# Fourier convolution of a 224 x 224 x 96 image: inverse transform of segments 6 and 7 regrouped, nine sums moved to GpSimd, four halo copies to ScalarE

## The chip, the cores and the metric

The kernel runs on one core of one Trainium2 chip. Its time is device time in microseconds (us) of one execution; the median over runs is compared. The engines are PE (TensorE, matmuls; its weight loads are listed as PEld), DVE (VectorE), ACT (ScalarE), POOL (GpSimd) and SP (SyncE, which only issues DMAs here). Each engine works through its own queue in order.

## The reference

```python
# x: (1, 224, 224, 96) bf16, w: (7, 7, 96, 96) bf16
wp = jnp.pad(w, ((0, H - K), (0, W - K), (0, 0), (0, 0)))
Xf = rfft2(x, axes=(1, 2)); Wf = rfft2(wp, axes=(0, 1))        # float32
Yf = jnp.einsum('bhwi,hwio->bhwo', Xf, Wf)
y = irfft2(Yf, s=(H, W), axes=(1, 2)).astype(bfloat16)
```

This is a circular convolution of the image with a 7 x 7 filter, 96 channels in and 96 out.

## The kernel before, in words

The 224 rows are cut into 8 segments (`NJ`) of 28 output rows (`B`), each with 6 rows of overlap, so 34 rows (`L`). Along the rows the kernel uses a transform of length 34, as matmuls with the matrix `Fm` (forward, step A) and `G` (inverse, step C). It has 17 frequencies (`NS`); a frequency has two parts (`r`), which gives `FR` = 34 rows of `G` per segment. Along the columns the 7-tap filter is applied directly to pairs of columns (step B). The 224 columns are cut into 7 tiles of 32 columns, that is 16 pairs (`TW`).

**Step A**, `a_jobs(t)`: for tile t, matmuls of image rows with `Fm` into a PSUM bank, then an evacuation into `xf` (two buffers, tile t uses t % 2). `new_xf` first copies the last three column pairs of the tile before into the new buffer, the halo, in two copies of 96 x 816 elements.

**Step B**, `b_round(t, s)`: one frequency s of one tile. 33 small matmuls (96 columns) go into two banks b0 and b1. ACT writes `tt_` from b0, DVE forms `u` and `v` from `tt_`, b0 and b1, and a last sum `yf = v + u` (`ysum`) runs on DVE if `ydve` is set, else on POOL. `u`, `v` and `tt_` have two buffers each, so a round can't write `u` before the sum two rounds back has read it. The operands of the matmuls are planes `J`, sums of parts of `xf` that `jit(t, g)` makes on DVE for a group of three frequencies at a time, in a *burst*: three DVE instructions that are put into one round (`planes`). Where the sum of a burst round is on POOL, it is made to wait for the last of the planes ("sum after planes").

**Step C**, `c_jobs(t)`: `yf` goes to a DRAM scratch `scr` (`put_y`), is read back as `tt` with rows (segment, frequency, part) and columns (pair, channel) (`load_t`), is multiplied by `G` and evacuated into `yo`, which is written to the output. Three segments make a group of 102 rows and 84 output rows (3 x 28); the 8 segments are the groups `CG` = (0, 3), (3, 3), (6, 2). A tile has two halves h of 8 pairs; each half and group takes four matmuls of two pairs (384 columns), so 24 matmuls per tile, two per bank pair in a job q. Loads and outputs are issued on SP, in program order; six `tt` buffers (`NTT`) are filled by `pump` as jobs are done.

**Order of the work.** The program is written out in Python, and each engine keeps the order of emission. The steps for the filter (`prep_jobs(gi)`, matmuls from `wq` whose results go to `WF`, and `w_sub`, a DVE subtraction on `WF`) and step A and C jobs are queued with a first and a last position (`add(a, b, jobs)`); `pace` pops them at two places of each round. In phase 1 tiles 0 and 1 go side by side: round r holds the *sub-rounds* (r, 0) for tile 0 with s = r, and (r, 1) for tile 1 with s = r - 4 (`LAG`). Bursts stand in (6, 0), (7, 1), (9, 0), (10, 1), (12, 0), (13, 1), (15, 0), (17, 1) and (19, 1), and before those in (4, 1) and earlier. From tile 2 on a tile runs alone, beside step A of the next tile and step C of the one or two before; `CQ[t]` tells how many jobs of the older and of the newer tile fall into tile t. `evac` chooses DVE or ACT for each evacuation by two counters `load["v"]` and `load["a"]`. The last tile (`TL`) ends in a tail with its own inverse matmuls `GA` and `GB`; the remaining jobs of tile 5 run at its start.

Nearly all instructions carry the line 82 of a helper in the profile, so they are told apart by their tiles.

Of the kernel before, what the change touches and what calls it, by code (L numbers as in the profile page):

```python
# [14 lines left out]
B = 28  # L15
# [7 lines left out]
TW = 16  # L23
HALO = 3
PXC = 16
# [12 lines left out]
LAG = 4  # L38
CQ = {2: (12, 2), 3: (10, 5), 4: (7, 8), 5: (4, 11), 6: (1, 6)}
NXN = 2  # L40
NP2 = 0
# [8 lines left out]
def kernel(  # L50
# [338 lines left out]
    def new_xf(t):  # L389
        xf = xf_bufs[t % 2]  # L390
        xf_tiles[t] = xf
        if t > 0:
            prev = xf_tiles[t - 1]
            for ph in range(2):
                r = VE.tensor_copy(out=xf[0:C, ph, :, :, 0:HALO, :].rearrange("c r s w j -> c (r s) (w j)"),
                                   in_=prev[0:C, ph, :, :, TW:TW + HALO, :].rearrange("c r s w j -> c (r s) (w j)"))
                apart(("A", t), "halo", r)
        return xf
# [188 lines left out]

    def load_t(t, gi, h):
        j0, nj = CG[gi]
        n = nj * FR  # L590
        tt = t_pool.tile([128, TW // 2, 2 * C], BF16, name="tt")
        tt_tiles[(t, gi, h)] = tt
        sv = scr_tiles[t].rearrange("w j s (r e) -> (j s r) w e", r=2)
        n0 = n // 16 * 16
        for (p0, p1) in ((0, n0), (n0, n)):
            dma(tt[p0:p1], sv[j0 * FR + p0:j0 * FR + p1, h * 8:(h + 1) * 8])
# [21 lines left out]

    def c_jobs(t):
        jobs = []  # L620
        for h in range(2):
            for gi in range(3):
# [3 lines left out]
                def mk_(q, h=h, gi=gi, j0=j0, nj=nj, hold=hold):  # L626
                    def f():
                        if q == 0:
                            hold["yo"] = yo_pool.tile([4 * B, PXC * C], BF16, name="yo")
                        tt = tt_tiles[(t, gi, h)]  # L630
                        yo = hold["yo"]
                        if True:
                            pc = psum_tile() if NP2 else None
                            for b in range(2):
                                pb = pc[:, b] if NP2 else bank()
                                TE.matmul(pb[0:nj * B, 0:4 * C], lhsT=G[0:nj * FR, 0:nj * B],
                                          rhs=tt[0:nj * FR, 4 * q + 2 * b:4 * q + 2 * b + 2, :].rearrange("p w e -> p (w e)"), start=True, stop=True)
                                if not NP2:
                                    evac(yo[0:nj * B, (2 * q + b) * 4 * C:(2 * q + b + 1) * 4 * C], pb[0:nj * B, 0:4 * C], 4 * C)
                            if NP2:  # L640
                              evac(yo[0:nj * B, q * 8 * C:(q + 1) * 8 * C].rearrange("p (b e) -> p b e", b=2), pc[0:nj * B, :, 0:4 * C], 8 * C)
                        if q == 1:
                            w0 = t * 2 * TW + h * PXC
                            dma(out[0, j0 * B:(j0 + nj) * B, w0:w0 + PXC, :].rearrange("h w c -> h (w c)"), yo[0:nj * B])
                            held[0] -= 1
                            pump()
                    return f
                for q in range(2):
                    jobs.append(mk_(q))
# [65 lines left out]
    qs = []  # L715
# [5 lines left out]
    for gi in range(1, len(PGRP)):  # L721
        b0 = PGRP[gi][0]
        add(max(0, 2 * b0 - 10), 2 * b0 - 4 if gi > 1 else 1, prep_jobs(gi) if gi > 1 else p1)
        for h, (r, t) in enumerate(((max(b0 - 4, 2), 1), (b0 - 2, 0)) if gi > 1 else ((0, 0), (0, 0))):
# [14 lines left out]
    for r in range(NS + LAG):  # L739
# [4 lines left out]
        for t in range(2):  # L744
# [8 lines left out]
            b_round(t, s, fills(qs, 2 * r + (t if both else 0)), fills(qs, 2 * r + (t if both else 1)), bool(now), now)  # L753
# [133 lines left out]
```

## Time and profile before

| | |
|---|---|
| median of 13 runs | 288.1 us (286.7 to 288.88) |
| profiled execution | 286.84 us |
| its span | 285.1 us |
| PE busy | 264.9 us (93%) |
| DVE busy | 242.1 us (85%) |
| ACT busy | 185.3 us (65%) |
| POOL busy | 87.5 us (31%) |

Groups of instructions in the part of the page that lists the costliest ones (busy us, mean ns of one):

| engine, output and input | count | busy | mean |
|---|---|---|---|
| PE, pb from WF, J | 2898 | 166.5 | 206 |
| POOL, yf from v, u | 75 | 75.4 | 1018 |
| ACT, xf from pb (96 x 408 and smaller) | 139 | 60.9 | 482 |
| ACT, yo from pb (84 x 384 and smaller) | 130 | 55.9 | 479 |
| PE, pb from tt, Gm | 144 | 35.6 | 328 |
| DVE, yf from v, u | 36 | 20.6 | 571 |
| DVE, copies xf from xf | 12 | 9.0 | 789 |

A matmul's mean is longer than what it holds PE for, since matmuls overlap in the pipeline; the busy column counts the overlap once. Arrows in the answers ("<-") name what ended an idle time.

### The profile page before, as it was taken

To read this page: it belongs to the slowest core of one execution; us is meant where nothing else is said; L and a number is where in the kernel's file an instruction comes from. 1 tells how busy PE (TensorE), PEld (TensorE's weight loads), DVE (VectorE), ACT (ScalarE), POOL (GpSimd) and SP (SyncE) were. 2 spreads that over 40 slices of the span, in tenths; PEclk is the share of its full clock that TensorE was granted. 3 is DMA by queue.
4 is the path that set the end of the run, shared out by engine and by line. 5 is a ranking of instruction groups with operands and counts; after the bars stand their busy time and mean duration, and the time that the engine had idled before them with its cause. 6 is when DMAs were issued, how large, how long until landed. Compare 5 with 4: busy or idle time off the path is not lost.

```text
span 285.1 us, 11562 instructions
## 1 busy us (share of the span) xinstructions
PE 264.9 (93%) x4822; PEld 236.2 (83%) x4822; DVE 242.1 (85%) x523; ACT 185.3 (65%) x460; POOL 87.5 (31%) x122
## 2 busy tenths in 40 slices
PE   8499998999968889999999999999999999889992
PEld 3198898999968889888989888899989888888661
DVE  6279999999899999988977799778997889988833
ACT  5079885756522856886888767987688875265523
POOL 2741001223423333332243313422332235343300
PEclk9979999999999999999999999999999999999979
DMA  8687242111121369998768773786759832596875
GB/s 162 109 225 194 44 143 76 46 44 44 47 84 44 110 208 187 236 281 259 216 165 236 212 231 95 157 217 181 216 202 220 223 100 85 156 209 191 218 202 180
DMA packets 44492, 46.01 MB, mean 161 GB/s; under 512 B 33458, under 2 KB 35182, under 8 KB 44344
## 3 DMA queue, kind: packets, MB, share of 16 engines
q1 hardware_dynamic: 44024, 43.78, 58.1%
q10 hardware_dynamic: 416, 1.49, 2.3%
q8 instruction: 38, 0.62, 1.0%
q14 instruction: 14, 0.11, 0.1%
HBM read 23.92 MB, written 21.33 MB: 159 GB/s over the span
## 4 chain that ended last, share of the span: by engine, by line
PE 52%; DVE 26%; DMA 7%; issue 5%; ACT 4%; POOL 2%; SPq 0%; DVEq 0%; POOLq 0%; ACTq 0%
PE pb L82 52%; DVE J L82 9%; DVE v L82 5%; DMA wq<-in_w_dram 4%; DVE xf L82 3%; DVE yf L82 3%; DVE WF L82 2%; POOL yf L82 2%; DVE u L82 2%; ACT xf L82 2%; DMA xn<-in_x_dram 2%; ACT WF L82 1%; DMA tt<-scr 1%; DVE yo L82 1%; SPq L82 0%
## 5 line engine op out<-in xcount | busy, mean ns | idle before, releaser
L82 PE MATMUL pb<-WF,J 96*128 96x96 bf16 x2898 | 166.5, 206 | 6.1 <-DVE J L82 5.4
L82 PEld LDWEIGHTS <-J 96*128 96x128 bf16 (+1 forms) x2910 | 142.0, 98 | 20.7 <-issue 8.7
L82 POOL TENSOR_TENSOR yf<-v,u 128x384 bf16<-128x384 f32 x75 | 75.4, 1018 | 162.7 <-issue 90.8
L82 ACT CAST xf<-pb 96x408 bf16<-96x408 f32 (+1 forms) x139 | 60.9, 482 | 6.9 <-PE pb L82 4.5
L82 PE MATMUL pb<-WF,xf 96*128 96x96 bf16 x952 | 60.1, 206 | 0.7 <-DVE WF L82 0.6
L82 ACT CAST yo<-pb 84x384 bf16<-84x384 f32 (+1 forms) x130 | 55.9, 479 | 4.7 <-PE pb L82 4.2
L82 DVE TENSOR_TENSOR J<-xf 96x1824 bf16<-96x1824 bf16 (+1 forms) x84 | 57.2, 720 | 0.1
L82 PEld LDWEIGHTS <-xf 96*128 96x128 bf16 x952 | 47.1, 98 | 1.0 <-issue 0.7
L82 PE MATMUL pb<-Fm,xn 118*128 118x136 bf16 x448 | 46.4, 222 | 1.2 <-DVE u L82 0.8
L82 PE MATMUL pb<-tt,Gm 102*84 102x384 bf16 (+1 forms) x144 | 35.6, 328 | 1.4 <-DMA tt<-scr 1.0
L82 ACT CAST WF<-pb 96x480 bf16<-96x480 f32 (+1 forms) x58 | 29.9, 581 | 10.1 <-PE pb L82 9.9
L82 PEld LDWEIGHTS <-xn 118*128 118x128 bf16 x448 | 30.0, 98 | 2.6 <-issue 1.9
L82 PE MATMUL pb<-wq 98*128 98x120 bf16 (+1 forms) x288 | 23.8, 234 | 4.4 <-DMA xn<-in_x_dram 4.4
L82 PEld LDWEIGHTS <-wq 98*128 98x128 bf16 x288 | 21.1, 151 | 4.9 <-issue 4.9
L82 DVE TENSOR_TENSOR J<-J 96x912 bf16<-96x912 bf16 (+1 forms) x42 | 25.0, 596 | 0.0
L82 DVE TENSOR_TENSOR yf<-v,u 128x384 bf16<-128x384 f32 x36 | 20.6, 571 | 1.2
L82 DVE CAST xf<-pb 96x408 bf16<-96x408 f32 (+1 forms) x33 | 15.6, 513 | 0.2 <-PE pb L82 0.2
L82 PEld LDWEIGHTS <-Gm 102*84 102x84 bf16 (+1 forms) x144 | 11.8, 113 | 4.5 <-DMA tt<-scr 1.1
L82 PE MATMUL pb<-wu 128*128 128x512 bf16 (+1 forms) x48 | 13.2, 448 | 1.1 <-DVE ct L82 1.1
L82 DVE CAST WF<-pb 96x480 bf16<-96x480 f32 (+1 forms) x14 | 8.5, 612 | 6.0 <-PE pb L82 5.6
L82 PEld LDWEIGHTS <-wu 128*128 128x128 bf16 (+1 forms) x48 | 6.5, 137 | 7.6 <-issue 2.8
L82 DVE COPY xf<-xf 96x816 bf16<-96x816 bf16 x12 | 9.0, 789 | 0.0
(390 smaller groups left out, 215.8 us busy)
## 6 DMA issues: line engine op xcount, KB each, us to landing
xn<-in_x_dram SPq DMA_DIRECT2D x13, 672.0 KB
scr<-yf SPq DMA_DIRECT2D x30, 288.0 KB
tt<-scr SPq DMA_DIRECT2D x24, 288.0 KB
out_dram<-yo SPq DMA_DIRECT2D x24, 252.0 KB
tt<-scr SPq DMA_DIRECT2D x12, 192.0 KB
out_dram<-yo SPq DMA_DIRECT2D x12, 168.0 KB
scr<-yf SPq DMA_DIRECT2D x6, 192.0 KB
scra<-yf SPq DMA_DIRECT2D x3, 288.0 KB
```

The costliest lines, as they stand in the source:

```text
L82: r = fn(*a, **k)
```

## The change

Five things are changed together.

- Step C of segments 6 and 7: a group of two segments over 8 pairs becomes one over 6 pairs in each half, with 68 rows. The remaining 34 rows of each `tt` tile are filled with parts of the pairs 12 to 15 of segments 6 and 7 (`REST`): in the first half segment 6, pairs 12 to 15, and segment 7, pairs 12 and 13; in the second half segment 7, pairs 14 and 15. So the first half has three matmuls of three segments, and the second one of three and two of two segments: 22 matmuls per tile instead of 24, and the third group is one job instead of two. Loads and outputs of the added parts are DMAs of their own, on SP.
- `CQ` is written for 10 jobs per tile instead of 12.
- The sums of burst rounds go to POOL for r >= 4 in phase 1, behind the planes.
- The halo copies of tiles 2 and 3 are on ACT, and all halo copies are counted in `load`.
- The filter jobs of group 5 and its two `w_sub` come two positions (one round) later.

```diff
@@ -36,7 +36,7 @@
 YBUF = 4
 JGB = ((0, 3), (3, 6), (6, 9), (9, 12), (12, 15), (15, 17))
 LAG = 4
-CQ = {2: (12, 2), 3: (10, 5), 4: (7, 8), 5: (4, 11), 6: (1, 6)}
+CQ = {2: (10, 2), 3: (8, 4), 4: (6, 7), 5: (3, 9), 6: (1, 5)}
 NXN = 2
 NP2 = 0
 WARM = 16
@@ -392,7 +392,9 @@
         if t > 0:
             prev = xf_tiles[t - 1]
             for ph in range(2):
-                r = VE.tensor_copy(out=xf[0:C, ph, :, :, 0:HALO, :].rearrange("c r s w j -> c (r s) (w j)"),
+                hc = SE.copy if t in (2, 3) else VE.tensor_copy
+                load["a" if t in (2, 3) else "v"] += 850 if t in (2, 3) else 600
+                r = hc(out=xf[0:C, ph, :, :, 0:HALO, :].rearrange("c r s w j -> c (r s) (w j)"),
                                    in_=prev[0:C, ph, :, :, TW:TW + HALO, :].rearrange("c r s w j -> c (r s) (w j)"))
                 apart(("A", t), "halo", r)
         return xf
@@ -585,6 +587,8 @@
     tt_tiles = {}
     puts = []
 
+    REST = (((6, 12, 16, 0), (7, 12, 14, 4)), ((7, 14, 16, 0),))
+
     def load_t(t, gi, h):
         j0, nj = CG[gi]
         n = nj * FR
@@ -592,8 +596,12 @@
         tt_tiles[(t, gi, h)] = tt
         sv = scr_tiles[t].rearrange("w j s (r e) -> (j s r) w e", r=2)
         n0 = n // 16 * 16
+        w0, w1 = (h * 8, (h + 1) * 8) if gi < 2 else (h * 6, (h + 1) * 6)
         for (p0, p1) in ((0, n0), (n0, n)):
-            dma(tt[p0:p1], sv[j0 * FR + p0:j0 * FR + p1, h * 8:(h + 1) * 8])
+            dma(tt[p0:p1, 0:w1 - w0], sv[j0 * FR + p0:j0 * FR + p1, w0:w1])
+        if gi == 2:
+            for j, wa, wb, q0 in REST[h]:
+                dma(tt[n:n + FR, q0:q0 + wb - wa], sv[j * FR:(j + 1) * FR, wa:wb])
 
     TW2 = 2 * TW * C
     tl_all = xf_bufs[(TL + 1) % 2].rearrange("c p r s w j -> c (p r s w j)")
@@ -616,6 +624,17 @@
                 dma(GB[KO[i] + j * n:KO[i] + (j + 1) * n, j // 4, j % 4 * B:(j % 4 + 1) * B], G[2 * s:2 * s1, 0:B])
                 yield
 
+    def c_bank(tt, yo, k, nj):
+        pb = bank()
+        TE.matmul(pb[0:nj * B, 0:4 * C], lhsT=G[0:nj * FR, 0:nj * B],
+                  rhs=tt[0:nj * FR, 2 * k:2 * k + 2, :].rearrange("p w e -> p (w e)"), start=True, stop=True)
+        evac(yo[0:nj * B, k * 4 * C:(k + 1) * 4 * C], pb[0:nj * B, 0:4 * C], 4 * C)
+
+    def put_o(t, yo, p0, j, nj, wa, wb, q0):
+        px = t * 2 * TW + 2 * wa
+        dma(out[0, j * B:(j + nj) * B, px:px + 2 * (wb - wa), :].rearrange("h w c -> h (w c)"),
+            yo[p0:p0 + nj * B, q0 * 2 * C:(q0 + wb - wa) * 2 * C])
+
     def c_jobs(t):
         jobs = []
         for h in range(2):
@@ -623,30 +642,29 @@
                 j0, nj = CG[gi]
                 hold = {}
 
-                def mk_(q, h=h, gi=gi, j0=j0, nj=nj, hold=hold):
+                def mk_(ks, done, h=h, gi=gi, j0=j0, nj=nj, hold=hold):
                     def f():
-                        if q == 0:
+                        if ks[0] == 0:
                             hold["yo"] = yo_pool.tile([4 * B, PXC * C], BF16, name="yo")
                         tt = tt_tiles[(t, gi, h)]
                         yo = hold["yo"]
-                        if True:
-                            pc = psum_tile() if NP2 else None
-                            for b in range(2):
-                                pb = pc[:, b] if NP2 else bank()
-                                TE.matmul(pb[0:nj * B, 0:4 * C], lhsT=G[0:nj * FR, 0:nj * B],
-                                          rhs=tt[0:nj * FR, 4 * q + 2 * b:4 * q + 2 * b + 2, :].rearrange("p w e -> p (w e)"), start=True, stop=True)
-                                if not NP2:
-                                    evac(yo[0:nj * B, (2 * q + b) * 4 * C:(2 * q + b + 1) * 4 * C], pb[0:nj * B, 0:4 * C], 4 * C)
-                            if NP2:
-                              evac(yo[0:nj * B, q * 8 * C:(q + 1) * 8 * C].rearrange("p (b e) -> p b e", b=2), pc[0:nj * B, :, 0:4 * C], 8 * C)
-                        if q == 1:
-                            w0 = t * 2 * TW + h * PXC
-                            dma(out[0, j0 * B:(j0 + nj) * B, w0:w0 + PXC, :].rearrange("h w c -> h (w c)"), yo[0:nj * B])
-                            held[0] -= 1
-                            pump()
+                        for k in ks:
+                            c_bank(tt, yo, k, 3 if gi < 2 or h == 0 or k == 0 else 2)
+                        if not done:
+                            return
+                        if gi < 2:
+                            put_o(t, yo, 0, j0, nj, 8 * h, 8 * h + 8, 0)
+                        else:
+                            put_o(t, yo, 0, j0, nj, 6 * h, 6 * h + 6, 0)
+                            for j, wa, wb, q0 in REST[h]:
+                                put_o(t, yo, nj * B, j, 1, wa, wb, q0)
+                        held[0] -= 1
+                        pump()
                     return f
-                for q in range(2):
-                    jobs.append(mk_(q))
+                if gi < 2:
+                    jobs.extend((mk_((0, 1), False), mk_((2, 3), True)))
+                else:
+                    jobs.append(mk_((0, 1, 2), True))
         return jobs
 
     NTT = 6
@@ -720,8 +738,8 @@
 
     for gi in range(1, len(PGRP)):
         b0 = PGRP[gi][0]
-        add(max(0, 2 * b0 - 10), 2 * b0 - 4 if gi > 1 else 1, prep_jobs(gi) if gi > 1 else p1)
-        for h, (r, t) in enumerate(((max(b0 - 4, 2), 1), (b0 - 2, 0)) if gi > 1 else ((0, 0), (0, 0))):
+        add(max(0, 2 * b0 - (10 if gi < 5 else 8)), 2 * b0 - (4 if gi < 5 else 2) if gi > 1 else 1, prep_jobs(gi) if gi > 1 else p1)
+        for h, (r, t) in enumerate(((max(b0 - 4, 2), 1), (b0 - 2, 0)) if 1 < gi < 5 else ((b0 - 3, 1), (b0 - 1, 0)) if gi == 5 else ((0, 0), (0, 0))):
             wsubs.setdefault((r, t if r >= LAG else 0), []).append(w_sub(gi, h))
     for t in range(2):
         scr_tiles[t] = dr_pool.tile([TW, NJ, NS, 4 * C], BF16, name="scr")
@@ -750,7 +768,7 @@
             if (r, t) in wsubs:
                 now = wsubs.pop((r, t)) + now if r < 1 else now + wsubs.pop((r, t))
             both = LAG <= r < NS
-            b_round(t, s, fills(qs, 2 * r + (t if both else 0)), fills(qs, 2 * r + (t if both else 1)), bool(now), now)
+            b_round(t, s, fills(qs, 2 * r + (t if both else 0)), fills(qs, 2 * r + (t if both else 1)), bool(now) and r < LAG, now)
     assert not wsubs and not bursts and nburst == 2 * len(JGB)
     if NP2:
         ps0_cm.__exit__(None, None, None)
```

## The prediction

> **What bounds the kernel now.** I read the page first (shares, slices), then busy time by stretches, then the waits of TensorE, then the timeline at the places that the diff touches.
>
> ```profile
> span 285.1 us, 11562 instructions
> PE 264.9 (93%) x4822; PEld 236.2 (83%) x4822; DVE 242.1 (85%) x523; ACT 185.3 (65%) x460; POOL 87.5 (31%) x122
> ...
> 60.00:80.00 20.00, 18.80 (x405) 18.41 (x403) 18.71 (x38) 11.50 (x28) 6.62 (x7) 1.00 0.16 62
> 80.00:100.00 20.00, 17.20 (x370) 16.78 (x371) 18.76 (x42) 9.20 (x24) 6.95 (x7) 1.00 0.23 75
> ...
> 180.00:200.00 20.00, 20.00 (x390) 18.08 (x387) 16.61 (x36) 16.27 (x43) 5.95 (x6) 1.00 0.78 202
> ```
>
> The stretches list busy time of PE, PEld, DVE, ACT and POOL in this order. There are two regimes. From about 110 to 245 us (tiles 2 to 5) PE is busy all the time and DVE is not: what is taken from PE there comes off the span. From 45 to 109 us (tiles 0 and 1 side by side: "phase 1") DVE has hardly a gap and PE stalls now and then. The stalls of PE, with the releaser behind the arrow, are few and add up to 5.4 us from 64 us on (0.38 us of it at 108.77, and 0.3 us in two small gaps at 64 and 70):
>
> ```profile
> 80.34 0.34 PE L82 MATMUL pb<-WF,J 96*128 96x96 bf16 x4 [1.48 <-DVE J L82]
> 85.88 0.34 PE L82 MATMUL pb<-WF,J 96*128 96x96 bf16 x4 [1.12 <-DVE J L82]
> 90.84 0.34 PE L82 MATMUL pb<-WF,J 96*128 96x96 bf16 x4 [0.58 <-DVE J L82]
> 95.74 0.69 PE L82 MATMUL pb<-Fm,xn 118*128 118x136 bf16 x9 [0.75 <-DVE u L82]
> 104.03 0.77 PE L82 MATMUL pb<-WF,J 96*128 96x96 bf16 x14 [0.73 <-DVE J L82]
> ```
>
> The last 12 us are a chain of DMAs (scratch written, read back, put out) that the change doesn't shorten.
>
> **The change, part 1: inverse matmuls.** Durations of single matmuls overlap, so I take start to next start:
>
> ```profile
> 115.98 0.49 PE L82 MATMUL pb<-tt,Gm 102*84 102x384 bf16 x2
> 116.31 0.34 PE L82 MATMUL pb<-WF,J 96*128 96x96 bf16 x4
> ...
> 121.65 0.51 PE L82 MATMUL pb<-tt,Gm 68*56 68x384 bf16 x2
> 122.09 0.77 PE L82 MATMUL pb<-WF,J 96*128 96x96 bf16 x14
> ```
>
> A pair of three segments (84 columns of weights) holds PE 0.33 us, a pair of two segments (56 columns) 0.44 us, and the same two numbers return wherever such a pair is followed at once by other matmuls. So the smaller form is the dearer one, and the change removes mostly that form. Per tile the third group costs 4 x 0.445 = 1.78 us before; after, four matmuls of three segments (4 x 0.165 = 0.66) and one pair of two (0.445): 1.11. Saved: 0.67 us per tile. Tiles 0 to 4: 3.37 us; the first half of tile 5 (1.78 / 2 - 3 x 0.165): 0.40 us; its second half runs in the tail beside the DMA chain: nothing. Sum 3.8 us. Off this I take 0.4 us, as the timeline has a few places among tiles 2 to 5 where PE waited 0.2 to 0.3 us for J behind such a pair (119.4, 142.3, 155.2), so that less PE work only shows the wait. The three matmuls now in one job take a third bank at once, which is only another order of the same evacuations; their number falls by 12, at about 0.48 us each, on engines with slack there. **-3.4 us** (2.4 to 3.9).
>
> **Part 2: the DMAs of it.** Per tile, loads go from 12 to 15 issues and outputs from 6 to 9, all on SP's queue (36 more), with the same bytes. Twelve loads held SP for 6.52 us in tile 6:
>
> ```profile
> 246.32 6.52 SPq L82 DMA_DIRECT2D tt<-scr  x12
> 252.94 0.40 SPq L82 DMA_DIRECT2D scra<-yf  x1
> ```
>
> Three more at 0.54 us make 1.6 us, which delays what stands behind: the write of scra at 252.94 (its next reader on SP starts at 260.68, and behind scra at 256.12) and, at 107 us in tile 2, a scratch write and the x load, used some 20 us later. The new pieces have 34 rows. By size alone they land within the 3.4 us that the chain shows for the first load of tile 6. The Trainium skill (DMA: Bandwidth & Descriptors, "Why a DMA increments its semaphore by 16 and not by 1") says that a DMA is spread on the largest number of engines up to 16 that divides the row count: 34 rows give 2, 96 rows give 16. Then the piece of 34 x 4 runs puts 68 runs on an engine where the large load puts 48, and I estimate 3.43 x 68/48 = 4.9 us. No run here shows such a piece yet. By the row it is there at about 254 us, by the rule at 255.6, and its first use is not before 257.3, where the pair of two segments stood: no cost by either, 1.7 us of margin by the rule. **0 us** (0 to +1).
>
> **Part 3: sums of burst rounds on GpSimd.** Nine sums (0.57 us each on DVE, 5 us) move. The timeline of one burst before, three sub-rounds long:
>
> ```profile
> 64.64 1.98 POOL L82 TENSOR_TENSOR yf<-v,u 128x384 bf16<-128x384 f32 x2 [3.95 <-DVE v L82]
> ...
> 65.67 0.36 DVE L82 SCALAR_TENSOR_TENSOR u<-pb,tt__1469 128x192 f32<-128x192 f32 x1 [0.38 <-POOL yf L82]
> 65.95 0.54 DVE L82 SCALAR_TENSOR_TENSOR v<-tt__1469,pb 128x384 f32<-128x384 f32 x1
> ...
> 66.53 0.56 DVE L82 TENSOR_TENSOR yf<-v,u 128x384 bf16<-128x384 f32 x1
> 67.00 1.40 DVE L82 TENSOR_TENSOR J<-xf 96x1824 bf16<-96x1824 bf16 x2
> ```
>
> u and v have two buffers each, so a u waits for GpSimd's sum of two rounds earlier (0.38 us here). After, the burst's own sum may start only behind its planes, at 63.9 us in this period, and takes 1.0 us. What waits then: the u of two sub-rounds later, which moves from 64.48 to 64.95; GpSimd's next sum runs to 65.9, the next u moves from 65.67 to 65.95, its v ends at about 66.8, and the third sum holds until 66.9. J would start at 66.8 to 66.95 instead of 67.00. So 0.47 us of DVE work goes and nearly as much waiting for GpSimd comes: three sums (3.0 us) and then the planes (J and WF, 2.75 us) are one ring of 5.8 us against 5.93. I take 0.1 us per burst, plus 0.48 us once at the first burst ((6, 0), at 54.65), where no such queue stands yet: 0.8 us by the burst of round (12, 0), and not more afterwards. The rule that speaks against this part is in the Trainium skill (SBUF — State Buffer, "Who interferes with whom"): a DVE instruction with two SBUF inputs and a GpSimd instruction shut each other out for their whole length. The row agrees:
>
> ```profile
> 239.21 2.94 POOL L82 TENSOR_TENSOR yf<-v,u 128x384 bf16<-128x384 f32 x2 [3.15 <-issue]
> ...
> 240.19 2.21 DVE L82 TENSOR_TENSOR J<-xf 96x1824 bf16<-96x1824 bf16 x2
> ```
>
> The two sums take 1.96 us elsewhere; here the second met a J, which took 2.21 us instead of 1.40. Without the lock J would gain another 0.1 us per burst (0.8 more in all); with it and a sum that only just started, a burst loses up to 0.8. The move of group 5's weights by two half rounds takes WF out of two bursts and gives GpSimd time to catch up; it is neutral in the same ring. **-0.8 us** (0 to -2.5).
>
> **Part 4: halo copies.** Four copies leave DVE; the two pairs stand at 93.90 (1.52 us) and 105.47 (1.45 us), both just before DVE is late (stalls at 95.74 and 108.77). On ACT I bound one between DVE's 0.79 us and twice a 408-element evacuation (0.96), and take 0.85: the pair delays what is behind it on ACT, the tt of the round and then the xf evacuations, by 1.6 us. ACT is full there too (10 casts in 3.86 us from 93.65). Tracing the order on: u of round (17, 1) comes 1.3 us earlier, but the next tt is behind nine casts, and the u after it gains only 0.45; the J for tile 2 gains 1.4 and the stall at 104.03 mostly goes, as does the 0.38 at 108.77. Past the 0.8 us of part 3, I keep **-0.9 us** (+1.0 to -1.9).
>
> Sum: -3.4 + 0 - 0.8 - 0.9 = -5.1 us, a span of 280.0. The profiled execution took 286.84, 1.3 below the median of 288.1; the difference is carried over to the median: **283.0 us**.
>
> **Rivals.**
> R1, only the matmuls count: in phase 1 waits for GpSimd and ACT eat everything. For it: the ring of 5.8 us; against: the stalls by J and u stand right behind the work that goes. -3.4: 284.7.
> R2, all PE stalls of phase 1 go (5.4) and all of the 3.8 counts: -9.2, 278.9. For it: DVE is full and loses 8 us of work; against: POOL's place in the ring and ACT at the tile switch.
> R3, slower: the lock. The burst's sum shifts GpSimd's queue by 1.0 us, so that its third sum has just started when J arrives, and J waits the whole of it. Price up to 0.9 us more than I count at each of 8 bursts: 7.2 - 5.1 = +2.1, 290.2. It decides from 0.64 us per burst on. Against: I find only 0.1 us of overlap.
> R4, no change: the 84-column matmuls gain nothing in the three-bank job (banks wait for evacuations) and phase 1 is as in R1: 288.
>
> **How the numbers follow.** Forecast 0.45, R1 0.22, R2 0.13, R4 0.07, R3 0.13. A measurement tells some 0.3% (0.9 us) from no change: faster 0.80, same 0.07, slower 0.13. The range leaves out the far ends of R2 and R4 and all of R3: 279.8 to 286.9.
>
> **What would show it.** Right: third-group matmuls at 0.165 us each in threes; PE still at 20.0 of 20 from 120 to 240 us, with tiles 2 to 5 some 3 us shorter in all; burst periods of 5.7 to 5.85 us with two waits of u for POOL; stalls at the first bursts' J of 0.5 to 0.9 us. Wrong: a J of over 2 us in bursts (R3); PE waiting for tt; PE idle at tile 2's start behind ACT's halo; three-bank jobs with gaps behind them.

## The result and the profile after

The changed kernel takes 283.54 us (median of 11 runs, 280.52 to 287.24), against 287.89 us for the kernel before, measured beside it (median of 48 runs). The ratio is 0.981, with a 95% interval of 0.977 to 0.984; of 287.89 us that is 5.6 us less. Executions more than 1.5% above the quickest of their kernel are left out of the ratios (four of after's twelve; the medians of all runs differ by 4.35 us), and the profiles of e7 and e8 below are of such executions. The forecast was 283.0. The profiled execution after took 280.04 us, less than any of the eleven, with a span of 278.2; of the 6.9 us between the two spans, 1.2 are there before any changed instruction has had an effect (table below). I therefore explain some 5.7 us.

The page after, with the stretches that were shown of before (busy time of PE, PEld, DVE, ACT, POOL; then the granted clock, the DMA share and GB/s):

```profile
span 278.2 us, 11572 instructions
PE 257.4 (93%) x4810; PEld 235.5 (85%) x4810; DVE 233.7 (84%) x502; ACT 185.6 (67%) x460; POOL 96.1 (35%) x131
...
60.00:80.00 20.00, 19.64 (x417) 19.03 (x414) 17.63 (x36) 10.77 (x25) 10.16 (x11) 1.00 0.13 48
80.00:100.00 20.00, 18.36 (x388) 17.77 (x387) 17.56 (x39) 11.75 (x31) 10.50 (x11) 1.00 0.32 107
...
180.00:200.00 20.00, 20.00 (x404) 18.66 (x402) 17.29 (x37) 15.70 (x43) 6.44 (x7) 1.00 0.67 183
```

In phase 1, DVE is now below 18 of 20 us, and PE has gained 0.8 and 1.2 us of work in the two stretches. In the steady tiles PE is not busy all the time any more, although the stretch shown is full: between the 36th and the 97th `u` of the table below it stands idle 1.76 us, against 0.47 before, mostly in two waits of 0.76 us (shown further down). Nine instructions more are on POOL.

**Where the time went.** A good clock for the stages is the start of `u`, a DVE instruction that each round but one of a tile issues once (16 per tile), as soon as PE has filled the round's bank. The 6th `u` is the last that nothing in the change can move; the 36th lies in tile 2, before the first inverse matmul; the 97th is the first of tile 6. All starts are read from the timeline of DVE. A star marks one of the three middle stages in which PE's granted clock was 0.50 for 3.4 or 6.8 us (in e6 without any effect); of the tail more is said below.

| kernel | start to 6th | 6th to 36th (phase 1) | 36th to 97th (tiles 2 to 5) | 97th to last (tile 6) | last to end (tail) | span |
|---|---|---|---|---|---|---|
| before | 52.60 | 61.75 | 128.52 | 23.99 | 18.24 | 285.1 |
| after | 51.44 | 58.87 | 124.93 | 23.58 | 19.38 | 278.2 |
| difference | -1.16 | -2.88 | -3.59 | -0.41 | +1.14 | -6.9 |
| e1, regrouping only | 51.78 | 61.74 | 125.01 | 23.47 | 21.70 | 283.7 |
| e2, all but the regrouping | 52.33 | 58.86 | 128.56 | 23.94 | 17.51 | 281.2 |
| e3, sums only | 52.89 | 60.37 | 128.52 | 27.09* | 17.33 | 286.2 |
| e4, halo copies only | 51.94 | 61.57 | 128.59 | 24.02 | 19.18 | 285.3 |
| e5, after, group 5 back | 52.18 | 58.79 | 124.17 | 23.69 | 20.47 | 279.3 |
| e6, before, 84 columns | 52.62 | 61.74* | 126.17 | 23.75 | 18.42 | 282.7 |
| e7, after, 84 columns | 52.79 | 58.84 | 128.65* | 23.72 | 18.90 | 282.9 |
| e8, after, sums don't wait for planes | 52.69 | 62.61 | 125.88 | 24.17 | 20.95 | 286.3 |
| e9, after, three u and v | 52.62 | 58.42 | 123.94 | 26.65* | 18.57 | 280.2 |
| e10, after, outputs later | 52.04 | 60.21* | 124.74 | 23.49 | 20.12 | 280.6 |
| e11, e10, jobs earlier | 51.24 | 58.87 | 127.56* | 23.81 | 20.52 | 282.0 |
| e12, e11, 84 columns | 52.13 | 58.83 | 124.37 | 23.44 | 21.13 | 279.9 |

Phase 1 repeats to 0.1 us from kernel to kernel with the same program there (58.83 to 58.87 in five of them), the first column doesn't (51.24 to 52.89 with one program). The spans are therefore the wrong thing to compare to a few tenths, and the stages are the right one.

Stalls of TensorE in phase 1, after (waits of PE, from the timeline):

```profile
78.08 0.34 PE L82 MATMUL pb<-WF,J 96*128 96x96 bf16 x4 [0.19 <-DVE J L82]
81.47 0.33 PE L82 MATMUL pb<-WF,xf 96*128 96x96 bf16 x4 [1.44 <-DVE WF L82]
```

Of the five stalls before, 4.66 us together, two are left, 1.63 us: 3.0 us less, which is about the 2.9 of the table.

The inverse matmuls of the third group, after, each with the matmul that follows (the timeline of PE; start, duration, then what):

```profile
118.10 0.65 PE L82 MATMUL pb<-tt,Gm 102*84 102x384 bf16 x3
118.59 0.33 PE L82 MATMUL pb<-WF,J 96*128 96x96 bf16 x4
...
127.70 0.77 PE L82 MATMUL pb<-tt,Gm 102*84 102x384 bf16 x3
128.40 0.34 PE L82 MATMUL pb<-WF,J 96*128 96x96 bf16 x4
```

The job of the first half holds PE for 0.49 us, 0.165 each, as forecast. That of the second half, which includes the pair of two segments, holds it 0.70 us and not the 0.61 that 0.165 and 0.445 give: its first matmul, just ahead of that pair, holds PE for 0.26 us. Per tile that is 1.19 us. The 1.78 us of the forecast leave such a price out; what it is comes with e6 below.

One burst, after (timeline of POOL and DVE, the lines that answer to the burst before):

```profile
61.97 2.93 POOL L82 TENSOR_TENSOR yf<-v,u 128x384 bf16<-128x384 f32 x3 [2.72 <-DVE WF L82]
63.01 0.36 DVE L82 SCALAR_TENSOR_TENSOR u<-pb,tt__1414 128x192 f32<-128x192 f32 x1 [0.38 <-POOL yf L82]
64.70 1.47 DVE L82 TENSOR_TENSOR J<-xf 96x1824 bf16<-96x1824 bf16 x2
...
67.67 2.95 POOL L82 TENSOR_TENSOR yf<-v,u 128x384 bf16<-128x384 f32 x3 [2.77 <-issue]
68.70 0.36 DVE L82 SCALAR_TENSOR_TENSOR u<-pb,tt__1558 128x192 f32<-128x192 f32 x1 [0.44 <-POOL yf L82]
69.68 0.36 DVE L82 SCALAR_TENSOR_TENSOR u<-pb,tt__1613 128x192 f32<-128x192 f32 x1 [0.16 <-POOL yf L82]
70.42 1.47 DVE L82 TENSOR_TENSOR J<-xf 96x1824 bf16<-96x1824 bf16 x2
```

POOL's three sums of a burst run without a gap between the planes, just as the ring in the forecast has them, and `u` waits for them once or twice. From J to J it is 5.72 us (5.94 before), and 5.66 to 5.90 in the first five periods. J takes 1.47 us for its two halves, against 1.40: the overlap with the third sum is there, and it is small in most bursts. Two later J pairs take 1.70 (76.32) and 1.76 us (102.91).

The halo copies on ACT, and what waits behind them:

```profile
89.78 1.63 ACT L82 COPY xf<-xf 96x816 bf16<-96x816 bf16 x2
...
99.93 1.63 ACT L82 COPY xf<-xf 96x816 bf16<-96x816 bf16 x2
```

```profile
91.83 0.36 DVE L82 SCALAR_TENSOR_TENSOR u<-pb,tt__2244 128x192 f32<-128x192 f32 x1 [0.25 <-ACT tt__2244 L82]
...
95.48 0.36 DVE L82 SCALAR_TENSOR_TENSOR u<-pb,tt__2337 128x192 f32<-128x192 f32 x1 [1.02 <-ACT tt__2337 L82]
```

A pair takes 1.63 us (1.6 was forecast to stand in ACT's way), `u` waits 1.3 us for ACT in all, and PE doesn't stall for it: the stalls of 0.75, 0.73 and 0.38 us at the tile switch are gone.

**What came back.** The queue of SP in the last tile, and the last sum on DVE (timeline):

```profile
238.68 9.94 SPq L82 DMA_DIRECT2D tt<-scr  x15
...
255.28 4.58 SPq L82 DMA_DIRECT2D out_dram<-yo  x4
259.90 0.37 SPq L82 DMA_DIRECT2D xf<-scrb  x1
259.94 0.56 DVE L82 TENSOR_TENSOR yf<-v,pb 128x384 bf16<-128x384 f32 x1
262.19 0.35 SPq L82 DMA_DIRECT2D scrb<-yf  x1
```

The fifteen loads hold SP for 9.94 us; twelve took 6.52, and I had forecast 8.1. The excess is not spread over them: three loads from 242.77 on, right behind the two small ones of the first half, take 3.52 us, the other twelve 0.53 each, as before. The last write of `scrb` starts 1.7 us after its sum is ready (260.50), although SP has issued the load before it by 260.27; before the change it started 0.03 us after the sum. The waits of SP between 258 and 263 us name what it stood for, a load from `scra` issued just after 254 us:

```profile
SPq L82 <- DMA xf<-scra: 1.9, 1, 1.9
```

The stretch from the last `u` to the end is 1.1 us longer. In the steady tiles PE waits twice: at the first `u` of tile 4, which stands on DVE behind a pair of halo copies and a J, and in tile 5 for a load of `tt` that came too late:

```profile
170.76 0.32 PE L82 MATMUL pb<-tt,Gm 102*84 102x384 bf16 x1 [0.76 <-DVE u L82]
...
211.62 0.49 PE L82 MATMUL pb<-tt,Gm 102*84 102x384 bf16 x2 [0.76 <-DMA tt<-scr]
```

The first of these waits (0.68 to 0.76 us) is there in all nine kernels with the regrouping and in none of the five without it.

### The profile page after: what moved, and what is told of

It reads as the page before. It is cut to its first block, busy times and chain, and to the rows that moved or that the text cites. A ratio compares the mean times of both kernels' runs of the same rounds, so it can differ in the third digit from the quotient of the medians.

```text
span 278.2 us, 11572 instructions
## 1 busy us (share of the span) xinstructions
PE 257.4 (93%) x4810; PEld 235.5 (85%) x4810; DVE 233.7 (84%) x502; ACT 185.6 (67%) x460; POOL 96.1 (35%) x131
## 4 chain that ended last, share of the span: by engine, by line
PE 63%; DMA 15%; DVE 9%; ACT 5%; issue 4%; POOL 1%; SPq 0%; DVEq 0%; ACTq 0%
PE pb L82 63%; DMA xn<-in_x_dram 4%; DMA wq<-in_w_dram 4%; ACT xf L82 3%; DMA tt<-scr 2%; DVE J L82 2%; DVE v L82 2%; DVE WF L82 2%; POOL yf L82 1%; DMA scrb<-yf 1%; DMA scr<-yf 1%; ACT WF L82 1%; DVE xf L82 1%; DMA xf<-scrb 1%; DVE u L82 1%
## 5 line engine op out<-in xcount | busy, mean ns | idle before, releaser
L82 POOL TENSOR_TENSOR yf<-v,u 128x384 bf16<-128x384 f32 x84 | 84.0, 1016 | 146.9 <-issue 96.7
L82 ACT CAST xf<-pb 96x408 bf16<-96x408 f32 (+1 forms) x143 | 62.0, 483 | 4.7 <-PE pb L82 2.6
L82 DVE TENSOR_TENSOR J<-xf 96x1824 bf16<-96x1824 bf16 (+1 forms) x84 | 58.6, 736 | 0.1
L82 ACT CAST yo<-pb 84x384 bf16<-84x384 f32 (+1 forms) x122 | 52.0, 483 | 9.7 <-PE pb L82 6.8
L82 PE MATMUL pb<-tt,Gm 102*84 102x384 bf16 (+1 forms) x132 | 32.2, 326 | 3.9 <-DMA tt<-scr 1.8
L82 DVE TENSOR_TENSOR yf<-v,u 128x384 bf16<-128x384 f32 x27 | 15.7, 582 | 0.9
L82 DVE CAST xf<-pb 96x408 bf16<-96x408 f32 (+1 forms) x29 | 14.5, 535 | 0.7 <-PE pb L82 0.6
L82 PE MATMUL pb<-wu 128*128 128x512 bf16 (+1 forms) x48 | 11.9, 414 | 1.0 <-DVE ct L82 1.0
L82 PEld LDWEIGHTS <-wu 128*128 128x128 bf16 (+1 forms) x48 | 5.6, 119 | 6.7 <-issue 2.8
L82 DVE CAST tt<-pb 112x384 bf16<-112x384 f32 x8 | 4.1, 554 | 5.9 <-PE pb L82 5.6
```

Of the source, the lines that this page charges most:

```text
L82: r = fn(*a, **k)
```

## The experiments

My theory: the regrouping is worth 3 to 4 us in tiles 2 to 5 and costs something at the end; sums and halo copies take the stalls of phase 1. The rivals: everything comes from the matmuls, or from phase 1; the lock between DVE and POOL decides what the sums are worth; and, within part 1, it is not the number of matmuls that counts, but that the 56-column form is hardly used any more.

**The regrouping alone, and all but the regrouping.** e1 is the changed kernel with these lines as before; e2 is the kernel before with these lines as after:

```diff
-                hc = SE.copy if t in (2, 3) else VE.tensor_copy
-                load["a" if t in (2, 3) else "v"] += 850 if t in (2, 3) else 600
-                r = hc(out=xf[0:C, ph, :, :, 0:HALO, :]...
+                r = VE.tensor_copy(out=xf[0:C, ph, :, :, 0:HALO, :]...
...
-            b_round(t, s, ..., bool(now) and r < LAG, now)
+            b_round(t, s, ..., bool(now), now)
...
-        add(max(0, 2 * b0 - (10 if gi < 5 else 8)), 2 * b0 - (4 if gi < 5 else 2) if gi > 1 else 1, ...)
+        add(max(0, 2 * b0 - 10), 2 * b0 - 4 if gi > 1 else 1, ...)
...
```

The line behind it, with the two `w_sub` of group 5, changes likewise.

> The kernel before with the regrouped inverse transform alone (REST, 10 jobs per tile, the new CQ). The forecast's part 1 and 2: -3.4 us, about 284.5 (ratio 0.988), all of it between tiles 2 and 5: the first planes of tile 6 come 3.2 to 3.4 us earlier than before, those of tile 2 at the same time. Rival (R4: three banks at once and the shorter loads eat it): 0 to -1 us. A second question is the tail: the changed kernel took 24.3 us from its last planes to the end where the kernel before took 23.1. If the added DMAs of tile 5 cause that, this kernel has 24 us or more there too; if it came with phase 1 or from chance, 23.1.

> The changed kernel without the regrouping: sums on GpSimd, halo copies on ACT, group 5 of the filter one round later. The forecast's parts 3 and 4: -1.7 us (ratio 0.994). The trace of the changed kernel says more: its planes of tile 2 stand 4.4 us earlier, 1.2 of it before any changed instruction. If that is phase 1 alone, this kernel is 3 us faster (0.990) and its planes of tile 2 stand 3 us or more earlier; the tail stays at 23.1 us.

Measured: e1 0.989 of the time before (0.985 to 0.994), e2 0.989 (0.984 to 0.995). The product is 0.978, inside the interval of the whole change. The stages part cleanly: e1 has the phase 1 of before (61.74) and tiles 2 to 5 shorter by 3.51; e2 has phase 1 shorter by 2.89 and tiles 2 to 5 unchanged (+0.04). Neither part needs the other. The tail is e1's loss: 21.70 us against 18.24, and 17.51 in e2.

**The form of the matmul.** e6 is the kernel before, still with 24 matmuls per tile, but with three segments' columns of weights for the pairs of two (the last 28 output rows are not read):

```diff
-    TE.matmul(pb[0:nj * B, 0:4 * C], lhsT=G[0:nj * FR, 0:nj * B], ...
+    TE.matmul(pb[0:3 * B, 0:4 * C], lhsT=G[0:nj * FR, 0:3 * B], ...
```

> The kernel before, with all 24 inverse matmuls per tile kept, but those of the third group with 84 columns of weights instead of 56; the added 28 output rows are not evacuated, so all other work is the same. If the 56-column form itself costs PE 0.11 us per pair, the four pairs of a tile save 0.45 us, and the 5.5 tiles on the path 2.5 us (ratio 0.991). If its price came from the 68 rows or from the loads of these tiles: no change.

Measured: 0.992 (0.989 to 0.995), tiles 2 to 5 shorter by 2.35 us. The pair, in the timeline of PE:

```profile
122.49 0.34 PE L82 MATMUL pb<-Fm,xn 118*128 118x136 bf16 x3
122.67 0.49 PE L82 MATMUL pb<-tt,Gm 68*84 68x384 bf16 x2
123.00 0.33 PE L82 MATMUL pb<-WF,J 96*128 96x96 bf16 x4
```

The pair with the same 68 rows holds PE 0.33 us instead of 0.44, just by having 84 columns of weights. So it isn't the rows: two thirds of what the regrouping gains in tiles 2 to 5 (2.35 of 3.51) is had by widening the weights alone, with no new DMA and no new grouping.

The pair is not the whole price of the form. Above, three matmuls with `Fm` hold PE for 0.18 us before the pair starts, 0.06 each. Before the change, two of them hold it for 0.21:

```profile
121.44 0.28 PE L82 MATMUL pb<-Fm,xn 118*128 118x136 bf16 x2
121.65 0.51 PE L82 MATMUL pb<-tt,Gm 68*56 68x384 bf16 x2
```

The first of the two holds it 0.06, the second, next to the 56-column pair, 0.15. It is the same ahead of all 20 such pairs between the 36th and the 97th `u`, whether a matmul with `Fm` stands there (0.15 for 0.06) or one with `J` (0.14 for 0.04). One 56-column pair thus costs some 0.21 us more than one with 84 columns: 0.11 in itself, 0.09 in the matmul ahead, 0.01 in the one behind. For 20 pairs that is some 4.2 us, of which e6 shows 2.35: PE's idle time grows by 0.84 us (1.31 for 0.47), and the rest stands in matmuls that hold PE a little longer than the same ones before. That these, too, are waits is likely and not shown.

e7 makes the same edit in the changed kernel, for the one pair per tile that is left.

> The changed kernel with the two matmuls per tile that still have 56 columns written with 84; the added rows are not evacuated. At 0.11 us per pair and tile: -0.6 us between the planes of tile 2 and those of tile 6 (129.65 to 129.1), which the total can hardly show (ratio to the changed kernel 0.998).

Measured: 0.976 (0.970 to 0.982); after has 0.981 (0.977 to 0.984). Up to the 85th `u`, before its clock sank, tiles 2 to 4 are 0.1 us shorter than after's. In e12, with the same edit, they are 0.3 us shorter. That is of the expected sign and less than expected, and the times don't tell it from nothing. In e7 a load of `tt` came 2.94 us too late in tile 5, and the half clock of that stage follows it.

**The sums alone, and the halo copies alone.** e3 is the kernel before with `bool(now) and r < LAG` in the call of `b_round`; e4 is the kernel before with the two lines of `hc` and `load` in `new_xf`.

> The kernel before with the nine sums on GpSimd alone. Ring theory (three sums and then the planes are one ring of 5.7 to 5.8 us): bursts 5.7 to 5.8 us apart instead of 5.94 while group 5 has two w_sub to do, and -0.8 to -1.5 us in all. Rival (the lock between a sum and a J decides, R3): J of 2 us or more in bursts and a time above the kernel before. Rival (DVE's 5 us come off in full): bursts 5.4 us apart, -3 us or more.

> The kernel before with the halo copies of tiles 2 and 3 on ACT (and halos counted in the evacuation's counters) alone. By difference of earlier traces the halos are worth 1.9 us of phase 1: planes of round (4, 1) to those of tile 2 take 58.2 us before and should take 56.3 to 56.8. The forecast had 0.9 us for it with the sums moved too: 57.3. If ACT behind them decides: 58 or more.

Measured: e3 0.991 (0.988 to 0.993), phase 1 shorter by 1.38; e4 0.994 (0.992 to 0.996), phase 1 shorter by 0.18. Together, in e2 and after, they give 2.89, and not 1.56. Where that comes from can be read round by round, as each `u` moves against the kernel before (both counted from the 6th `u`; us):

| | 25th | 28th | 30th | 32nd | 33rd | 36th |
|---|---|---|---|---|---|---|
| sums (e3) | -0.96 | -1.19 | -1.30 | -2.07 | -1.38 | -1.38 |
| halo copies (e4) | -0.03 | -0.02 | +0.57 | +0.58 | -0.18 | -0.18 |
| both, and group 5 (after) | -1.01 | -1.25 | -1.33 | -2.36 | -2.88 | -2.88 |

The sums alone have gained 2.07 us by the 32nd `u` and lose 0.69 of it again at the 33rd. Between the two, in e3 (timeline of POOL and DVE):

```profile
103.18 2.08 POOL L82 TENSOR_TENSOR yf<-v,u 128x384 bf16<-128x384 f32 x2 [3.36 <-issue]
103.70 2.15 DVE L82 COPY xf<-xf 96x816 bf16<-96x816 bf16 x2
```

The halo pair of tile 3 takes 2.15 us on DVE, against 1.45 before. Neither is what the copies take alone. That can be read off the pair for tile 1, where no sum is near (before, DVE):

```profile
28.56 0.64 DVE L82 COPY xf<-xf 96x816 bf16<-96x816 bf16 x2
```

In the kernel before, one sum meets the pair and the second copy ends only 0.2 us behind the sum; here two sums stand in a row and each copy ends behind one of them. DVE has no other gap in this stretch, and the 0.70 us is the loss. With the copies on ACT the sums meet just a J there, of 1.76 us for 1.40 (102.91 in after). The other way round, the halo copies alone make the 30th `u` later by 0.57, as it waits for ACT, on which the halo pair and then ten evacuations stand ahead of `tt` (e4, timelines of ACT and DVE):

```profile
91.79 1.63 ACT L82 COPY xf<-xf 96x816 bf16<-96x816 bf16 x2
93.32 0.41 ACT L82 ACTIVATE tt__2244<-pb 128x288 f32<-128x288 f32 x1
93.62 3.85 ACT L82 CAST xf<-pb 96x408 bf16<-96x408 f32 x10
97.29 0.49 ACT L82 ACTIVATE tt__2337<-pb 128x288 f32<-128x288 f32 x1
```

```profile
97.88 0.36 DVE L82 SCALAR_TENSOR_TENSOR u<-pb,tt__2337 128x192 f32<-128x192 f32 x1 [1.33 <-ACT tt__2337 L82]
```

With the sums on POOL, `b_round` adds 900 and not 1460 to DVE's counter, and `evac` gives one of the ten to DVE (in e2, nine casts of 3.44 us stand here); at the 30th `u` nothing of the 0.57 is left. So the two edits each cover the weak place of the other, and the price of either alone says little about the pair. That the counters cause the shift of the evacuation is read from the code; it was not tried by itself. Nor was ACT for the halo pairs of tiles 4 to 6, which meet two sums each and take 1.8 us on DVE in every kernel.

**Group 5's weights.** e5 is the changed kernel with the two lines on `gi < 5` and `gi == 5` as before.

> The changed kernel with the filter jobs of group 5 and their two w_sub where they stood before. In the changed kernel PE waits 1.44 us for WF at 81.47, and that WF was moved to round (13, 0) by the change. If the move costs that, phase 1 (planes of round (4, 1) to those of tile 2) shrinks from 54.96 us to 53.6 to 54.4. Rival: WF back in the bursts delays the planes, and PE waits for J in its place: 55 to 56 us. In the forecast's ring: no difference.

Measured: 0.976 (0.971 to 0.980); phase 1 58.79 against 58.87. The move is neutral, as forecast, but it changes which wait there is. PE in e5 (stalls in the timeline):

```profile
78.79 0.34 PE L82 MATMUL pb<-WF,J 96*128 96x96 bf16 x4 [0.92 <-DVE J L82]
84.09 0.34 PE L82 MATMUL pb<-WF,J 96*128 96x96 bf16 x4 [0.88 <-DVE J L82]
88.81 0.34 PE L82 MATMUL pb<-WF,J 96*128 96x96 bf16 x4 [0.34 <-DVE J L82]
```

Three waits for J, 2.1 us, stand where after has one for WF (1.44) and one for J (0.19). DVE is late in both; only the operand that comes last is another one.

**The lock.** e8 takes out the wait of a burst's sum for the planes:

```diff
-                if last is not None:
-                    tc.add_manual_dep(y.ins, last.ins.name, SYNC, reason="sum after planes")
```

> The changed kernel without the rule that a burst's sum waits for the planes: the sum may start as soon as v is there, while the planes run. Lock theory: the first J waits for a whole sum, the two J together take 2.4 us instead of 1.47, but no u waits for the burst's own sum; bursts 5.9 us apart instead of 5.7, phase 1 longer by 1 to 2 us. If sum and planes could run side by side: J stays at 1.4 us and phase 1 is shorter by up to 2 us. It holds for the bursts of tiles whose sum is on GpSimd only.

Measured: phase 1 takes 62.61 us, 3.7 more than after and 0.9 more than before, at a granted clock of 1.00; the ratio of the whole is 0.986 (0.982 to 0.990), some 1.6 us more than after's 0.981, and the median of all 14 runs, 286.76 us, is 3.2 above after's. POOL, DVE and PE in bursts of e8 (timeline):

```profile
65.34 3.79 POOL L82 TENSOR_TENSOR yf<-v,u 128x384 bf16<-128x384 f32 x3 [2.42 <-DVE v L82]
67.10 2.27 DVE L82 TENSOR_TENSOR J<-xf 96x1824 bf16<-96x1824 bf16 x2
69.43 0.34 PE L82 MATMUL pb<-WF,J 96*128 96x96 bf16 x4 [1.11 <-DVE J L82]
...
73.31 2.29 DVE L82 TENSOR_TENSOR J<-xf 96x1824 bf16<-96x1824 bf16 x2
```

J takes 2.27 us instead of 1.47, and the three sums 3.79 instead of 2.93: each holds the other up by some 0.8 us. The bursts are 6.2 us apart. This is the mechanism of my rival R3, at the price that it named (up to 0.9 per burst), and it needs the sum to run beside the planes. In the changed kernel the wait forbids this for the burst's own sum, and the ring leaves just 0.07 us of it for the third sum in most bursts, 0.3 at 76.32.

**The waits in the ring.** e9 has three buffers of `u` and of `v` in place of two (and five of `tt` instead of six, for the space):

```diff
-    NTT = 6
+    NTT = 5
+    uv_pool = ctx.enter_context(tc.tile_pool(name="uv", bufs=3))
-            u = tv_pool.tile([128, 2, C], F32, name="u")
-            v = tv_pool.tile([128, 2, 2, C], F32, name="v")
+            u = uv_pool.tile([128, 2, C], F32, name="u")
+            v = uv_pool.tile([128, 2, 2, C], F32, name="v")
```

> The changed kernel with three buffers each for u and v instead of two; to make room, five tt buffers instead of six, which can slow tiles 2 to 6 but not phase 1. Ring theory: DVE's waits for GpSimd in phase 1 go (0.4 to 0.8 us per burst in the changed kernel), and phase 1 shrinks from 54.96 us until PE is the bound, to 53 to 54.5 us. If the waits were only slack: 54.9.

Measured: 0.979 (0.974 to 0.984), phase 1 58.42, 0.45 less than after. The waits of `u` for POOL are gone, and DVE's idle time in phase 1 falls from 6.2 to 2.3 us, but J takes up nearly all of it: its instructions keep DVE busy for 25.14 us there, against 21.56 in after. One burst of e9 (timelines of POOL and DVE):

```profile
63.15 2.91 POOL L82 TENSOR_TENSOR yf<-v,u 128x384 bf16<-128x384 f32 x3 [2.71 <-DVE WF L82]
65.19 2.15 DVE L82 TENSOR_TENSOR J<-xf 96x1824 bf16<-96x1824 bf16 x2
```

J is now issued while the third sum still runs, and takes 2.15 us for 1.47. From J to J it is 5.6 to 5.7 us, as in after (the next starts at 70.81). The wait has only moved from `u` into J: three sums and then the planes remain one ring, which the lock closes where the buffers no longer do. The wait for WF is the same 1.44 us.

**The tail.** e10 issues the two added outputs of tile 5's first half later, behind the second load for `GB`, to let the last write of `scrb` go in time. e11 has this and starts tile 5's remaining jobs two positions earlier. e12 is e11 with the 84 columns of e7.

```diff
+                                if t == TL - 1 and h == 0:
+                                    rest5.append(f2)
+                                else:
+                                    f2()
...
     load_b(2, DE, 1)
+    for f in rest5:
+        f()
...
-        k1 = 2 * NS if t < TL else 2 * NS - 9
+        k1 = 2 * NS if t < TL else 2 * NS - 11
```

> The changed kernel with two of the added outputs of tile 5 (segment 6 and 7, first half) put on SP's queue behind the last read of scrb instead of ahead of it. In the changed kernel the last scratch write was issued 1.7 us after its sum, in the run with the regrouping alone 3.2 us after, and in both SP waited 1.7 to 1.9 us for the load of xf from scra; in the program that write waits for the completion of the DMA eight issues earlier, and the added outputs make that one the load of scra. If so, the write follows its sum within 0.1 us here, PE's wait for xf from scrb (2.04 us) shrinks, and the tail takes 22.5 to 23.3 us instead of 24.3: -1 to -1.8 us. If the tail is long for another cause (traffic of the small outputs): 24 us.

> The kernel with two added outputs of tile 5 put off behind the last read of scrb, and with the five jobs of tile 5 in tile 6 spread over ten positions instead of twelve. In the changed kernel the second job pair's output fell behind the loads of scra on SP, in the kernel before it stood ahead of them; the evacuations of the tail then wait for its yo buffer, PE stalls 0.6 to 2.5 us, and in four of six runs with the regrouping PE's clock was at half in the next stretch. If this is what gives back the tail: no PE wait for yo over 0.3 us in the tail, and from the last planes to the end 22.2 to 23.3 us, as in the four runs without the regrouping, instead of 23.8 to 26.6; -1.5 to -2.5 us against the changed kernel. If the small outputs as such cost it: 24 or more.

> The same tail as in the kernel with ten positions, and the last 56-column matmuls with 84 columns. If both hold: 2 to 3 us below the changed kernel, a ratio to the kernel before of 0.971 to 0.975.

Measured: e10 0.980 (0.973 to 0.986), e11 0.981 (0.977 to 0.985), e12 0.983 (0.978 to 0.987): none is faster than the changed kernel. In e10 the late write is mended, 0.03 us after its sum, and SP's wait for the load from `scra` is gone; the tail is 20.12 us all the same (19.38 in after). Timeline of e10:

```profile
261.59 0.55 DVE L82 TENSOR_TENSOR yf<-v,pb 128x384 bf16<-128x384 f32 x1
262.17 0.35 SPq L82 DMA_DIRECT2D scrb<-yf  x1
...
264.59 1.76 PE L82 MATMUL pb<-xf,GA 72*112 72x384 bf16 x5 [1.15 <-ACT yo L82]
```

PE stands for `yo`, as it did in after (1.11 and 0.60 us), since ACT waits 1.80 us for an output to leave its buffer; and PE's granted clock is 0.50 from 264.1 to 270.9 us, so that the 16 matmuls that keep PE warm take 5.10 us and not 2.77. In e11 the wait for `yo` is gone, and PE stands for the loads of `scra` instead:

```profile
264.52 0.83 PE L82 MATMUL pb<-xf,GA 72*112 72x384 bf16 x4 [0.83 <-DMA xf<-scra]
267.39 1.25 PE L82 MATMUL pb<-xf,GA 72*112 72x384 bf16 x4 [2.04 <-DMA xf<-scra]
```

So two causes that I could name were removed one after the other, and the time did not come back. Over all kernels, the stretch from the last `u` to the end is 20.2 us on the mean of the nine with the regrouping (18.57 to 21.70) and 18.1 on the mean of the five without it (17.33 to 19.18), one execution each. That the regrouping gives back about 2 us there is shown; what in it does so is shown in part. The loss lies ahead of the first matmul with `GB`: from there to the end it is 9.2 to 9.7 us in all kernels but e12 (10.9).

For the profiled pair it can be followed. In after the last write of `scrb` starts 3.4 us after the last `u`, in before 1.7, and the `GB` matmuls, which need it read back, start 10.05 us after the last `u` and not 8.86: that is the 1.1 us. The write is late by 1.4 to 3.2 us in five of the six regrouped kernels without the edit of e10 (not in e9), and by 0 to 0.4 in the three with it; of the five without regrouping, only e4 has it late, by 1.1. In e10 the write is in time, and PE is at half clock in its place. Granted clock, waits for `yo` and loads can't be separated further here: the half clock comes in tails with PE waits of 1 to 2.5 us (e1, e5, e8, e10) and also in before, where PE waited nowhere above 0.2 us and the 16 matmuls took 4.24. A tail with tile 5 in the old grouping would settle it and was not tried.

## Why the prediction was right, and which of its steps were not

The time was right to 0.5 us, and the sum hides mistakes each way; that they cancel is luck.

**Part 1, the matmuls, -3.4 us.** The mechanism was right, and the size came out of two errors that cancel. Tiles 2 to 5 gained 3.59 and tile 6 0.41; e1 alone gives 3.51 and 0.52. The start-to-start price of a pair (0.33 and 0.44) carried the forecast, and e6 shows that it is a price of the form: with 84 columns the old pairs cost 0.33. "The smaller form is the dearer one" could have been turned into the cheaper edit, which gets two thirds of it. But the price begins one matmul earlier than I took it (0.09 us a pair). With it the third group costs some 2.15 us per tile before and 1.19 after, so five tiles save 4.8 us of PE's work and not 3.4; PE's busy time from the 36th to the 97th `u` falls by 4.9 (128.05 to 123.17). Off that go 1.3 us of new idle time (1.76 for 0.47), where I took 0.4 for waits for J: it is mostly the `u` at tile 4 and the load of `tt`, neither of which I had. My sign "PE still at 20.0 of 20" therefore held in a part of the stretches only, and "PE waiting for tt", which I had put among the signs of being wrong, came once.

**Part 2, the DMAs, 0 us.** This is the step that failed. I placed the three more loads at 0.54 us each and looked for the first reader behind them, where I found a margin of 1.7 us. In fact fifteen took 9.94 us, 3.4 more than twelve and not 1.6; in tile 5 the loads of `tt` come late in six of the nine regrouped kernels (0.76 us in after, 2.94 in e7, 1.79 in e11, 1.37 in e8, 0.51 in e12, 0.21 in e10; nothing in e1, e5 and e9), and in none of the five others; and the tail is 1.1 us longer in this execution and 2 on the mean. "The last 12 us are a chain of DMAs that the change doesn't shorten" was true, and I didn't ask whether it lengthens it. The tail alone is already past the upper end of this term, +1. The rule of the Trainium skill on the number of engines per DMA (DMA: Bandwidth & Descriptors, "Why a DMA increments its semaphore by 16 and not by 1") was neither confirmed nor refuted: no run isolates the landing of a piece of 34 rows.

**Part 3, the sums, -0.8 us.** The ring was right in its form (three sums and the planes without a gap, one or two waits of `u`, 5.66 to 5.90 us from J to J against the forecast's 5.7 to 5.85), and subtracting its waits nearly one to one was right too: e9 takes the waits out, and J grows by nearly as much. The gain up to the burst of (12, 0) is near the forecast (0.96 at the 25th `u` in e3), but "and not more afterwards" was wrong: the sums alone have 2.07 us by the 32nd. Why the later ones bring more I have not traced. The rule that speaks against this part, the lock of the Trainium skill (SBUF — State Buffer, "Who interferes with whom"), holds here wherever a J is issued into a running sum: 0.8 us per burst and 3.7 us in phase 1 in e8. It holds for the halo copies too, which have one input and which I had not applied it to: a pair of 0.64 us takes 1.45 with one sum and 2.15 with two. In most bursts of the changed kernel it is kept out by the order, not by luck.

**Part 4, the halo copies, -0.9 us.** Behind the sums they are worth 1.5 us (2.88 less 1.38), by themselves 0.2. The forecast followed the order on from the kernel with the sums moved, and was right that the J of tile 2 and the 0.38 at 108.77 go. It took DVE's 0.79 us per copy for work, where more than half of it is waiting for a sum (0.32 alone), and so its estimate of 0.85 for ACT, bounded by that figure, is right in part by luck (0.82 measured). And it didn't see that the moved sum would meet the copies on DVE, so that taking them away also saves 0.7 us of lock. Parts 3 and 4 together: -1.7 forecast, -2.9 measured.

**Group 5, neutral.** Right (58.79 and 58.87), with a different operand to wait for.

So the terms were -3.4, 0, -1.7, and are about -4.0 (with the late load of `tt` in it), +1.1 and -2.9 in the profiled pair. R1 (only the matmuls, 284.7) falls by e2, R2 (all stalls go) by the 1.6 us of stalls that are left and by the tail, R4 by the 0.165 us per matmul. R3 is not what happened; its lock appears at full price in e8, where phase 1 is longer than before, though even there the whole stays faster than before.

## What to carry to other kernels

Before regrouping work to save a few matmuls, price each form from start to next start in the stream in which it stands, and begin at the matmul ahead of it: here a matmul with 56 columns of weights was dearer than one with 84, nearly half of the difference stood in its neighbour, and padding it gave two thirds of the gain with no DMA added. Before taking a mean duration for the price of an instruction, find one that meets nothing: the halo copies had 0.79 us on the mean and 0.32 alone. When work is split into more DMAs on a queue that ends the kernel, price the last tile by itself: every issue there stands before the final write or takes a share of what it needs. And price edits that fill each other's gaps (sums to POOL, copies off DVE) as a pair, by following one order of work with both in it; alone, either one may show next to nothing.

## What the runs showed of the hardware that I had not expected

- The same 68 rows and 384 elements take 0.33 us per pair with 84 columns of weights, and 0.44 with 56, between other matmuls whose weights have 128 columns; and the matmul ahead of a 56-column pair holds PE 0.09 us longer. No run here tells why.
- DVE and POOL delay each other by nearly the whole overlap: a J pair of 1.47 us becomes 2.27 and three sums of 2.93 become 3.79 in the same burst (e8). Copies with a single input are held up as well: a pair of 0.64 us alone takes 1.45 when one sum meets it (before) and 2.15 with two (e3).
- A DMA can be held at the issue although its data are ready: the last write of `scrb` stood 1.7 us, and SP's waits name a load from `scra`, which has no data in common with it. Moving two outputs that had nothing to do with either let it go at once (e10), as expected from the program, in which an issue waits for the DMA eight issues earlier.
- Three more loads held the issuing queue by 3.4 us more: twelve of the fifteen took 0.53 us each, as before, and three in a row 3.52. What those three waited for was not found.
